# Spare products dropped, one copy moved and three tiles shifted at the start of a performer attention with a Mish network

## The chip, the cores and the metric

One Trainium2 chip, one core. The metric is the device time of one execution in microseconds, the median of several runs. The engines are TensorE (PE, matrix products), VectorE (DVE), ScalarE (ACT), GpSimd (POOL) and SyncE (SP), whose queue issues most of the transfers.

## The reference

Attention with random features ("performer"), 8 batches of 8 heads, 576 positions, 64 wide, 128 features; its output, one row of 512 for each of 4608 tokens, goes through a network with one hidden layer of 2048 and the activation Mish.

```python
def phi(x):
    h = einsum('bhsd,md->bhsm', x, omega) - sum(x * x, -1, keepdims=True) / 2.0
    return exp(h - max(h, -1, keepdims=True)) / sqrt(m)
q_p, k_p = phi(q * scale), phi(k * scale)
kv = einsum('bhsm,bhsd->bhmd', k_p, v)         # sums over the keys of a batch
num = einsum('bhsm,bhmd->bhsd', q_p, kv)
den = einsum('bhsm,bhm->bhs', q_p, sum(k_p, axis=2)) + 1e-06
x = (num / den) as 4608 x 512
out = mish(x @ w_in) @ w_out                   # mish(h) = h * tanh(log(1 + exp(h)))
```

## The kernel before, in words

The work is a stream of generators. Keys are handled by batch and pair of heads (`k_task`, tiles named k0_0 to k7_3), queries by tiles of 128 tokens (`q_task`, q0 to q35), both through `features`; the network goes by chunks of 256 tokens: `ff_in` for the first layer (PE tiles ph, 16 blocks of f each as ph chunk_group_quarter_pair), `ff_out0` and `ff_out` for the second (po). Weights arrive in eight blocks each (`w_task`), as raw words that ACT (Prelu), POOL and DVE turn into float32; a cast on ACT and a remainder on DVE (`w_split`) then give two float16 parts. `agenda` holds all generators with the slot at which they go on; `step` moves on to the next slot, and `yield n` puts a generator n slots back. What is written in that order is then placed by the Tile framework's scheduler, which gives every engine its order; `tc.high_priority(PRIO)` lets instructions be placed ahead of others. So a `yield 1` decides which rows stand beside each other, and the scheduler may move further ones.

The first tiles are special. Batches 0 and 1 and tiles 0 to 4 are computed in float32 (`whole`): ACT takes the exponentials straight from PSUM with `mx` as bias (L402), key sums are copied from PSUM into `kvf` (L461, by ACT), and `q_first` transposes the queries' features (pt, L581), copies them (qp, L584), multiplies them with the key sums (pn, L592) and divides (x, L599 or L605). Tiles 0 and 1 are transposed by PE (px, L616) into xT for chunk 0; tiles from 2 on are split (xs) and transposed by a DMA on SP (`x_parts`, L569). Tile 4 goes this way too; tiles from 5 on use float16 features in two parts (sq on ACT and POOL, pq L376 on PE, maxima and differences on DVE, exponentials L412 on ACT, qn on ACT and DVE, a transposing DMA to qp L525, pn L540).

`spin` (L97) puts products on PE that nobody reads. Thirteen of them open the kernel; `features` puts one or two behind the exponentials of the first tasks, counted by `nth` (0 to 3 are batch 0's keys, 4 and 5 are q0 and q1), and `q_first` puts two ahead of tile 0's last transposes.

Chunk 0's first layer leaves its sums in g (copied from ph by ACT), and `mish0` applies Mish to each half of g in place, 128x2048 at a time, the second half first as written. ACT must load a table of functions when it goes from exponentials or Prelu to Mish or back; these rows are ACT_TABLE_LOAD.

Transfers on SP go out in their order of issue. A load into a buffer waits until the last reader of that buffer is done: f buffers of tag `af` (queries and keys) rotate by two, raw buffers share the tag `g` with the hidden layers.

Of the kernel before, what the change touches and what calls it, by code (L numbers as in the profile page):

```python
# [15 lines left out]
AF = mybir.ActivationFunctionType  # L16
# [14 lines left out]
def tile_kernel(  # L31
# [17 lines left out]
    FT = DF // P  # L49
# [298 lines left out]
    def features(load, tiles, name, nth, whole):  # L348
# [61 lines left out]
        yield gap("exp", name)  # L410
        if not by_act:
            last = act.activation(e, e, AF.Exp, bias=lnt)  # L412
        elif nth < 6 and nth not in (2, 3):
            spin(2 if nth > 3 else 1, ident, e[:, 0:2, :].rearrange("p n m -> p (n m)"))
        anchors[nth] = anchors["e"] = (last.ins, sub.ins)
        return e

# [19 lines left out]
    def k_task(nth, b, hp):  # L437
# [8 lines left out]
        if b < KF:  # L446

            yield gap("kv", f"k{b}_{hp}")
            vt = vts[b]
            pkv = (ps_o if nth < 4 else ps_a).tile(  # L450
                [P, 2, D1], F32, tag="o" if nth < 4 else "a", name=f"pkv{b}_{hp}", padded_shape=[P, 2, 256]
            )
            for j in range(2):
                for i, (t, u) in enumerate(steps[j]):
                    nc.tensor.matmul(  # L455
                        out=pkv[:, j, :], lhsT=e[:, t, :], rhs=vt[hp][:, u, :],
                        start=i == 0, stop=i == 4,
                    )
            yield 1
            f = kvf[b][:, 2 * hp:2 * hp + 2]  # L460
            cast(act, f, pkv)  # L461
            did("kvf", b)
            yield 4
            if (b * S + S - 1) // P >= QF and hp == HP - 1:
                must(HP, "kvf", b)
                start(kv_parts(b, kvf[b], kv[b]))
            return
# [105 lines left out]

    def q_first(nth, t, e, off):

        qp = sb.tile([P, H, P], F32, tag="ap", name=f"qp{t}", bufs=2)
        for g in range(2):
            hs = slice(4 * g, 4 * g + 4)
            pt = ps_a.tile([P, 4, P], F32, tag="a", name=f"pt{t}_{g}")
            for i in range(4):  # L580
                nc.tensor.transpose(out=pt[:, i, :], in_=e[:, 4 * g + i, :], identity=ident)  # L581
            cast(act, qp[:, hs, :], pt)
        yield 1
        x = sb.tile([P, H, D], F32, tag="x", name=f"x{t}", bufs=2)  # L584
        rd = sb.tile([P, H, 1], F32, tag="rd", name=f"rd{t}")
        for g in range(2):
            hs = slice(4 * g, 4 * g + 4)
            pn = ps_a.tile([P, 4, D1], F32, tag="a", name=f"pn{t}_{g}", padded_shape=[P, 4, P])
            for i in range(4):
                for b, lo, hi in spans(t * P, P):  # L590
                    must(HP, "kvf", b)
                    nc.tensor.matmul(  # L592
                        out=pn[lo:hi, i, :], lhsT=qp[:, 4 * g + i, lo:hi], rhs=kvf[b][:, 4 * g + i, :],
                        start=True, stop=True,
                    )
            dve.tensor_single_scalar(out=rd[:, hs], in_=pn[:, :, D:D1], scalar=EPS, op=ALU.add)
            dve.reciprocal(out=rd[:, hs], in_=rd[:, hs])
            if t * P < CH:
                xt = dve.tensor_tensor(  # L599
                    out=x[:, hs, :], in0=pn[:, :, 0:D], in1=rd[:, hs].broadcast_to([P, 4, D]),  # L600
                    op=ALU.mult,
                )
                continue
            for b, lo, hi in spans(t * P, P):
                xt = dve.scalar_tensor_tensor(  # L605
                    out=x[lo:hi, hs, :], in0=pn[lo:hi, :, 0:D], scalar=vstate[b][2][lo:hi],
                    in1=rd[lo:hi, hs].broadcast_to([hi - lo, 4, D]), op0=ALU.mult, op1=ALU.mult,
                )
        anchors[30 + t] = (xt.ins,)
        if t * P >= CH:  # L610
            yield from x_parts(nth, t, x)
            return
        yield 1
        px = ps_a.tile([P, KT, P], F32, tag="a", name=f"px{t}")
        for i in range(KT):
            nc.tensor.transpose(out=px[:, i, :], in_=x[:, 2 * i:2 * i + 2, :], identity=ident)  # L616
        anchors[40 + t] = (cast(act, xT0()[:, :, off:off + P], px).ins, xt.ins)
        if off == 0:
            spin(2, ident, x[:, 0:4, :].rearrange("p h d -> p (h d)"))
        did("x0")  # L620


# [48 lines left out]
    def ff_in(c):  # L671
# [5 lines left out]
        for gr in range(FT // FG):  # L677
            gT[c, gr] = sb.tile([P, 2, FG, CH], F16, tag="g", name=f"g{c}_{gr}", bufs=GB)
            for q in range(FG // FQ):
# [4 lines left out]
                for j in range(0, FQ, 2):  # L684
# [11 lines left out]
                            )  # L696
                    if c == 0:

                        later(1, cast, act, h[:, j:j + 2, :], ph)
                        if gr == FT // FG - 1 and q == FG // FQ - 1 and j > 0:  # L700
                            later(2, mish0)
                    else:
# [53 lines left out]
    def mish(sp, h, ph):  # L756

        for us, lo, hi in sp:
            anchors["h"] = act.activation(h[:, :, lo:hi], ph[:, :, lo:hi], AF.Mish, scale=us[:, 0:1]).ins  # L759

    def mish0():
        for gr in reversed(range(FT // FG)):
            act.activation(g0(gr), g0(gr), AF.Mish)
            for q in range(FG // FQ):
                did("g", 0, q)

# [79 lines left out]
    def gap(what, name):  # L846
        if name in ("k0_0", "k0_1", "k0_2", "k0_3", "q0", "q1"):
            return GAP0[what]
        return GAP[what]

    def pace(c):
# [205 lines left out]
```

## Time and profile before

| | us |
|---|---|
| median of 3 runs (lowest to highest) | 938.64 (938.16 to 938.83) |
| the profiled execution | 937.79 |
| its span | 936.0 |
| PE busy, share of the span | 921.6, 98% |
| ACT busy | 628.5, 67% |
| DVE busy | 529.6, 57% |
| POOL busy | 231.1, 25% |

The profiled execution is one run, its span the time between the first and the last recorded instruction. Times below are from the span's start. A row of a timeline can hold several instructions of one form (xN) with its start, the time from the first's start to the last's end, and in brackets the idle time of the engine ahead of it and what ended that. Products in float32 leave two or more records each.

### The profile page before, as it was taken

The page shows a single profiled execution, that of the slowest core. Times are in us where ns is not written, and L with a number is a line of the kernel's source. Part 1 is how long each engine was busy: PE and PEld are TensorE (multiplying, and loading weights), DVE is VectorE, ACT ScalarE, POOL GpSimd, SP SyncE. Part 2 cuts the span into 40 slices and gives each one's busy share as a digit, 9 for nine tenths or more (in the row PEclk, how much of TensorE's full clock was granted, in tenths as well). Part 3 has the DMA queues.
Part 4 walks back from the last instruction along what each step waited for, and adds up shares of the span by engine and source line. Part 5 has one row for each costly group of instructions (what it writes and reads, how often), then busy time and mean ns, then how long its engine had stood idle before and what let it go on. Part 6 is the DMA issues. An engine that isn't in the chain of part 4 may idle for free.

```text
span 936.0 us, 16681 instructions
## 1 busy us (share of the span) xinstructions
PE 921.6 (98%) x6797; PEld 532.4 (57%) x6797; DVE 529.6 (57%) x1019; ACT 628.5 (67%) x914; POOL 231.1 (25%) x143
## 2 busy tenths in 40 slices
PE   9998999999999999999999999999999999999998
PEld 6886866777655555555555555555555555444443
DVE  3899779855646784577357753784476345201200
ACT  5769998996949954897388747963887268304401
POOL 1331143541432233313232232323332121000000
PEclk9999999999999999999999999999999999999999
DMA  9975334623531256214531264203430242101001
GB/s 284 327 210 180 112 70 96 119 86 71 133 94 37 52 122 122 61 28 98 109 89 38 47 128 120 49 24 77 117 50 23 46 113 43 37 1 46 1 1 45
DMA packets 128204, 82.05 MB, mean 88 GB/s; under 512 B 106432, under 2 KB 106560, under 8 KB 128128
## 3 DMA queue, kind: packets, MB, share of 16 engines
q1 hardware_dynamic: 127392, 79.47, 34.1%
q10 hardware_dynamic: 736, 1.52, 0.6%
q8 instruction: 53, 0.87, 0.4%
q14 instruction: 23, 0.19, 0.1%
HBM read 46.37 MB, written 9.44 MB: 60 GB/s over the span
## 4 chain that ended last, share of the span: by engine, by line
PE 89%; DVE 5%; ACT 4%; issue 1%; DMA 0%; POOL 0%; ACTq 0%; DVEq 0%; POOLq 0%
PE po L745 31%; PE ph L721 31%; PE po L787 6%; PE ph L692 5%; PE pq L376 3%; PE pk L376 2%; PE pkv L490 2%; PE pn L540 2%; PE pkv L455 2%; PE po L804 1%; PE spin L97 1%; DVE wmax L213 1%; DVE w L207 1%; PE pk L391 1%; ACT ek L402 1%
## 5 line engine op out<-in xcount | busy, mean ns | idle before, releaser
L721 PE MATMUL ph<-xT,w 128*128 128x512 f16 x1344 | 298.4, 379 | 0.0
L745 PE MATMUL po<-wo,gp 128*128 128x512 f16 x1344 | 296.9, 379 | 0.0
L745 PEld LDWEIGHTS <-gp 128*128 128x128 f16 x1344 | 129.5, 98 | 149.9
L721 PEld LDWEIGHTS <-w 128*128 128x128 f16 x1344 | 129.1, 98 | 148.2
L82 DVE SCALAR_TENSOR_TENSOR gp<-h,us,gp 128x256 f16<-128x256 f32 (+6 forms) x104 | 103.7, 1013 | 121.9 <-ACT gp L69 121.6
L759 ACT ACTIVATE h<-ph,us 128x128 f32<-128x128 f32 (+6 forms) x240 | 108.0, 502 | 46.5 <-PE ph L721 42.4
L78 POOL TENSOR_TENSOR sq<-fq,sq 64x1024 f16<-64x1024 f32 x31 | 67.0, 2163 | 213.9 <-ACT sq L69 118.0
L692 PE MATMUL ph<-xT,w 128*128 128x256 f16 (+2 forms) x720 | 96.4, 290 | 1.3 <-DMA xT<-xs 0.8
L69 ACT ACTIVATE o<-po,us 128x512 f32<-128x512 f32 (+1 forms) x38 | 25.9, 682 | 98.9 <-PE po L745 92.5
L78 POOL TENSOR_TENSOR xs<-x,xs 128x512 f16<-128x512 f32 x34 | 46.0, 1353 | 157.0 <-issue 80.0
L78 POOL TENSOR_TENSOR sk<-fk,sk 64x1152 f16<-64x1152 f32 x24 | 58.3, 2431 | 90.2 <-ACT sk L69 90.1
L397 DVE TENSOR_REDUCE mxk<-pk 128x4 f32<-128x512 f32 (+1 forms) x96 | 49.9, 549 | 45.9 <-PE pk L376 33.4
L69 ACT ACTIVATE gp<-h,us 128x256 f16<-128x256 f32 (+6 forms) x104 | 73.8, 755 | 0.3
L397 DVE TENSOR_REDUCE mxq<-pq 128x4 f32<-128x512 f32 x72 | 46.6, 680 | 43.6 <-PE pq L376 39.5
L787 PE MATMUL po<-wo,g 128*128 128x512 f16 x288 | 65.4, 379 | 0.0
L78 DVE TENSOR_TENSOR qn<-eq,qn 128x1024 f16<-128x1024 f32 x31 | 39.1, 1262 | 43.0 <-ACT qn L69 43.0
L692 PEld LDWEIGHTS <-w 128*128 128x128 f16 x576 | 55.5, 98 | 10.9 <-issue 2.4
L759 ACT ACT_TABLE_LOAD x43 | 55.2, 1283 | 0.8
L69 ACT ACTIVATE sq<-fq 64x1024 f16<-64x1024 f32 x31 | 32.7, 1055 | 31.4 <-issue 29.9
L412 ACT ACT_TABLE_LOAD x39 | 50.0, 1283 | 0.7
L78 DVE TENSOR_TENSOR kp<-ek,kp 128x1152 f16<-128x1152 f32 x24 | 33.9, 1414 | 25.1 <-ACT kp L69 25.1
L78 POOL TENSOR_TENSOR vb<-vf,vb 128x640 f16<-128x640 f32 x24 | 35.9, 1499 | 46.3 <-DVE vb L71 34.5
(127 smaller groups left out, 1063.1 us busy)
## 6 DMA issues: line engine op xcount, KB each, us to landing
vf<-in_vL_dram SPq DMA_DIRECT2D x30, 325.0 KB, 3.2
out_dram<-o SPq DMA_DIRECT2D x36, 256.0 KB, 2.3
fq<-in_qT_dram SPq DMA_DIRECT2D x31, 256.0 KB, 3.4
fk<-in_kT_dram SPq DMA_DIRECT2D x24, 256.0 KB, 3.6
raw<-in_w_out_dram SPq DMA_DIRECT2D x5, 1024.0 KB, 7.1
wo<-in_w_in_dram SPq DMA_DIRECT2D x4, 1024.0 KB, 12.3
raw<-in_w_in_dram SPq DMA_DIRECT2D x4, 1024.0 KB, 14.6
wo<-in_w_out_dram SPq DMA_DIRECT2D x3, 1024.0 KB, 8.3
```

Source lines behind the costliest of these rows:

```text
L69: return act.activation(out, in_, AF.Copy, scale=scale)
L78: ins = eng.tensor_tensor(out=out, in0=in_, in1=hi, op=ALU.subtract)
L82: return eng.scalar_tensor_tensor(out=out, in0=in_, scalar=scale, in1=hi, op0=ALU.mult, op1=ALU.subtract)
L376: nc.tensor.matmul(out=pp[:, i, :], lhsT=left[:, o:o + P], rhs=right, start=j == 0, stop=j == len(terms) - 1,)
L397: sub = dve.tensor_reduce(out=mx[:, lo:hi], in_=pp[:, :m, :], axis=AX.X, op=ALU.max, negate=by_act)
L412: last = act.activation(e, e, AF.Exp, bias=lnt)
L455: nc.tensor.matmul(out=pkv[:, j, :], lhsT=e[:, t, :], rhs=vt[hp][:, u, :], start=i == 0, stop=i == 4,)
L692: ff_mm[0] = nc.tensor.matmul(out=ph[:, i, part], lhsT=wi(a, k, f) if c else wi0(k, f), rhs=x_two(c // 2)[:, y, k, lo:lo + CH] if c else x ...
L721: ff_mm[0] = nc.tensor.matmul(out=ph[:, 0, :], lhsT=wi(a, k, f), rhs=x[:, y, k, :], start=n == 0, stop=n == len(mm) - 1,)
L745: ff_mm[0] = nc.tensor.matmul(out=po[i], lhsT=gP[g, gr][:, a, f % FQ, i * P:(i + 1) * P], rhs=wo(y, f), start=f == 0 and (a, y) == parts[0 ...
L759: anchors["h"] = act.activation(h[:, :, lo:hi], ph[:, :, lo:hi], AF.Mish, scale=us[:, 0:1]).ins
L787: ff_mm[0] = nc.tensor.matmul(out=po[i], lhsT=gT[c, f // FG][:, a, f % FG, i * P:(i + 1) * P], rhs=wo(y, f), start=f == order[0] and (a, y ...
```

## The change

Five edits. Tiles' products that nobody reads: `features` keeps one spin behind k0_0 and k0_1 and none behind q0 and q1, and `q_first` none ahead of tile 0's last transposes. The sum pkv0_3 of batch 0's last pair of heads is copied by DVE (`nth == 3`). `q_first` waits a step for t above 1, which holds for tiles 2, 3 and 4 (tiles 0 and 1 are not touched; tile 4 is the last that uses it). Tile 6's gap ahead of its products is 3 instead of 2. Chunk 0's Mish stands under high priority, as does the copy that fills the last block of its input, and the half of group 1 is done in two pieces of 128x1024.

```diff
-        elif nth < 6 and nth not in (2, 3):
-            spin(2 if nth > 3 else 1, ident, e[:, 0:2, :].rearrange("p n m -> p (n m)"))
+        elif nth < 2:
+            spin(1, ident, e[:, 0:2, :].rearrange("p n m -> p (n m)"))
...
-            cast(act, f, pkv)
+            cast(dve if nth == 3 else act, f, pkv)
...
     def q_first(nth, t, e, off):
 
+        if t > 1:
+            yield 1
...
-        if off == 0:
-            spin(2, ident, x[:, 0:4, :].rearrange("p h d -> p (h d)"))
         did("x0")
...
-                        later(1, cast, act, h[:, j:j + 2, :], ph)
+                        last = gr == FT // FG - 1 and q == FG // FQ - 1
+                        later(1, urgent if last else cast, act, h[:, j:j + 2, :], ph)
...
+    def urgent(*args):
+        with tc.high_priority(PRIO):
+            cast(*args)
+
     def mish0():
+        with tc.high_priority(PRIO):
+            mish0_()
+
+    def mish0_():
         for gr in reversed(range(FT // FG)):
-            act.activation(g0(gr), g0(gr), AF.Mish)
+            for q in ((1, 0) if gr else (slice(None),)):
+                w = g0(gr)[:, q * FQ:(q + 1) * FQ] if gr else g0(gr)
+                act.activation(w, w, AF.Mish)
...
         if name in ("k0_0", "k0_1", "k0_2", "k0_3", "q0", "q1"):
             return GAP0[what]
+        if what == "lo" and name == "q6":
+            return 3
         return GAP[what]
```

What the scheduler makes of it is seen in the built order of the engines. The first place is ACT around chunk 0's second Mish and the exponentials of batch 1's first keys (ek_0 is k1_0, ek_1 is k1_1, w_105 to w_109 are casts of weight blocks, raw_791 and raw_822 are Prelu). Before, from the cast that stands behind all of k1_0's exponentials:

```order
L69 ACTIVATE w_105<-w_106,s_w_656 128x1024
L198 ACTIVATE raw_791<-raw_791 128x1024
L402 ACTIVATE ek_1_824<-pk_1_5_828,mxk_1_825 128x128 x3
L69 ACTIVATE w_106<-w_107,s_w_656 128x1024
L402 ACTIVATE ek_1_824<-pk_1_0_826,mxk_1_825 128x128 x4
L402 ACTIVATE ek_1_824<-pk_1_5_828,mxk_1_825 128x128
L402 ACTIVATE ek_1_824<-pk_1_4_827,mxk_1_825 128x128
L69 ACTIVATE g_1_706<-ph_1_1_2_809 128x512
L69 ACTIVATE w_107<-w_108,s_w_656 128x1024
L198 ACTIVATE raw_822<-raw_822 128x1024
L763 ACT_TABLE_LOAD
L763 ACTIVATE g_1_706<-g_1_706 128x2048
```

And now, from the copy that is urgent:

```order
L69 ACTIVATE g_1_694<-ph_1_1_2_797 128x512
L69 ACTIVATE w_105<-w_106,s_w_644 128x1024
L774 ACT_TABLE_LOAD
L774 ACTIVATE g_1_694<-g_1_694 128x1024
L69 ACTIVATE w_106<-w_107,s_w_644 128x1024
L402 ACT_TABLE_LOAD
L402 ACTIVATE ek_0_760<-pk_0_0_762,mxk_0_761 128x128
L69 ACTIVATE w_107<-w_108,s_w_644 128x1024
L402 ACTIVATE ek_0_760<-pk_0_0_762,mxk_0_761 128x128 x2
L402 ACTIVATE ek_0_760<-pk_0_5_764,mxk_0_761 128x128 x4
L69 ACTIVATE w_108<-w_109,s_w_644 128x1024
L402 ACTIVATE ek_0_760<-pk_0_4_763,mxk_0_761 128x128
```

Mish moved ahead of eight of the nine exponentials of k1_0, with a table load on each side, and three casts between; the other piece of Mish stands further up, behind Mish of the other half. On PE the second layer of chunk 0 moved with it: four products po stand ahead of the rest of k1_1's products, three more behind the first pkv of batch 1, and then those of k1_2.

The second place is SP around tile 4's queries (fq_1069 before, fq_1058 now) and raw0 (raw_928, now raw_917); what an instruction waits for stands in brackets. Before:

```order
L170 DMA raw_898<-in_w_out_dram 128x2x512 [waits DMAHW6_49,DVE_49]
L321 DMA fq_1069<-in_qT_dram 64x512 [waits DMAHW2_49,DMAHW7_49,DMAHW1_49,PE_49]
L321 DMA fq_1069<-in_qT_dram 64x512 [waits DMAHW0_49]
L170 DMA raw_928<-in_w_out_dram 128x2x512 [waits DVE_49]
L290 DMA vf_2_1525<-in_vL_dram 128x650 [waits PE_49]
```

Now:

```order
L170 DMA raw_886<-in_w_out_dram 128x2x512 [waits DMAHW6_49,DVE_49]
L321 DMA fq_1058<-in_qT_dram 64x512 [waits DMAHW2_49,DMAHW7_49,DMAHW1_49,PE_49]
L170 DMA raw_917<-in_w_out_dram 128x2x512 [waits DMAHW0_49,DVE_49,Activation_49]
L321 DMA fq_1058<-in_qT_dram 64x512
L290 DMA vf_2_1514<-in_vL_dram 128x650 [waits PE_49]
```

raw0 went ahead of the second half of the queries and stands behind the first as before, whose wait on PE is for the products of k1_2, the last readers of its buffer.

The third place is ACT at tile 4 (eq its exponentials, qp the copies of its transposed features, sq the high part of tile 5's queries). Before:

```order
L402 ACT_TABLE_LOAD
L402 ACTIVATE eq_1111<-pq_0_1113,mxq_1112 128x128 x4
L402 ACTIVATE eq_1111<-pq_4_1114,mxq_1112 128x128 x4
L69 ACTIVATE g_0_867<-h_0_1_1027,us_862 128x1024
L69 ACTIVATE qp_1182<-pt_0_1183 128x512
L69 ACTIVATE qp_1182<-pt_1_1189 128x512
L759 ACT_TABLE_LOAD
L759 ACTIVATE h_1_0_1127<-ph_1_0_0_1128,us_862 128x512
L69 ACTIVATE sq_1252<-fq_1124 64x1024
L759 ACTIVATE h_1_0_1127<-ph_1_0_2_1196,us_862 128x512
```

Now:

```order
L402 ACT_TABLE_LOAD
L402 ACTIVATE eq_1100<-pq_0_1102,mxq_1101 128x128 x4
L402 ACTIVATE eq_1100<-pq_4_1103,mxq_1101 128x128 x4
L69 ACTIVATE g_0_855<-h_0_1_1016,us_850 128x1024
L760 ACT_TABLE_LOAD
L760 ACTIVATE h_1_0_1116<-ph_1_0_0_1117,us_850 128x512
L69 ACTIVATE sq_1210<-fq_1113 64x1024
L69 ACTIVATE qp_1197<-pt_0_1198 128x512
L69 ACTIVATE qp_1197<-pt_1_1204 128x512
L760 ACTIVATE h_1_0_1116<-ph_1_0_2_1172,us_850 128x512
```

The two copies moved behind a table load, a Mish and sq. On PE tile 4's products with the key sums (pn) stand ten products into the following block of the first layer instead of ahead of it, one product po more stands ahead of tile 5's pn, and half a block of chunk 1's second layer ahead of chunk 2's first product. Without the edit at tile 6 the built order is the same.

## Rows read from the trace of the kernel before

**Rows 1.** The page: its first line, and the granted clock of PE in 40 equal slices, in tenths of full speed (9 is 90% or more).

```profile
span 936.0 us, 16681 instructions
PEclk9999999999999999999999999999999999999999
```

**Rows 2.** Busy time by stretches: the stretch in us, its length, then busy time (and instructions) of PE, PE's weight loads, DVE, ACT, POOL, the granted clock, the mean busy share of the DMA engines, GB/s.

```profile
20.00:30.00 10.00, 10.00 (x95) 9.22 (x95) 4.91 (x7) 9.81 (x30) 4.21 (x4) 1.00 1.05 386
...
40.00:50.00 10.00, 8.73 (x73) 6.64 (x71) 9.86 (x24) 7.12 (x22) 0.52 (x1) 1.00 0.90 288
50.00:60.00 10.00, 10.00 (x60) 9.15 (x59) 10.00 (x20) 5.64 (x9) 2.88 (x2) 1.00 0.39 127
...
80.00:90.00 10.00, 8.10 (x70) 6.66 (x68) 9.19 (x12) 9.95 (x16) 0.00 (x0) 1.00 0.67 218
...
150.00:160.00 10.00, 9.16 (x85) 7.09 (x83) 9.86 (x28) 9.91 (x12) 4.46 (x2) 1.00 0.54 123
...
180.00:600.00 420.00, 420.00 (x3360) 237.26 (x3359) 259.47 (x507) 314.11 (x426) 125.70 (x71) 1.00 0.37 83
```

**Rows 3.** The waits of PE in the first 200 us, each with its line and with what ended it: us in total, times, the longest.

```profile
PE po L804 <- ACT g L763: 1.8, 1, 1.8
PE pk L376 <- DVE x L556: 1.6, 1, 1.6
PE spin L97 <- DVE idle L92: 1.5, 1, 1.5
PE pq L376 <- POOL sq L78: 1.5, 1, 1.5
PE pt L581 <- ACT eq L402: 1.3, 1, 1.3
PE pk L391 <- ACT ek L402: 1.1, 1, 1.1
PE ph L692 <- DMA xT<-xs: 0.8, 1, 0.8
```

**Rows 4.** The timeline of PE: start, time from the first's start to the last's end, line, operation, tiles and shapes.

```profile
27.21 1.03 PE L97 MATMUL spin<-eq,ident 128*128 128x256 f32 x4
...
29.64 3.24 PE L592 MATMUL pn<-kvf,qp 128*128 128x65 f32 x28
...
76.56 1.52 PE L391 MATMUL pk<-om_f,fk 64*128 64x128 f32 x18 [1.13 <-ACT ek L402]
...
80.10 2.34 PE L455 MATMUL pkv<-vf,ek 128*128 128x65 f32 x20
82.54 1.78 PE L391 MATMUL pk<-om_f,fk 64*128 64x128 f32 x20
...
88.84 5.42 PE L804 MATMUL po<-wo,g 128*128 128x512 f32 x12 [1.80 <-ACT g L763]
...
119.89 1.15 PE L592 MATMUL pn<-kvf,qp 128*64 128x65 f32 x32
...
154.80 2.75 PE L787 MATMUL po<-wo,g 128*128 128x512 f16 x12
```

**Rows 5.** The timeline of ACT.

```profile
75.90 1.64 ACT L402 ACTIVATE ek<-pk,mxk 128x128 f32<-128x128 f32 x6
77.48 1.15 ACT L69 ACTIVATE w<-w,s_w 128x1024 f16<-128x1024 f32 x1
...
85.58 1.28 ACT L763 ACT_TABLE_LOAD   x1
86.88 1.91 ACT L763 ACTIVATE g<-g 128x2048 f32<-128x2048 f32 x1
...
99.09 2.19 ACT L198 ACTIVATE raw<-raw 128x1024 f32<-128x1024 f32 x2
...
116.94 1.09 ACT L69 ACTIVATE qp<-pt 128x512 f32<-128x512 f32 x2 [0.25 <-PE pt L581]
...
119.34 0.69 ACT L759 ACTIVATE h<-ph,us 128x512 f32<-128x512 f32 x1
119.92 1.04 ACT L69 ACTIVATE sq<-fq 64x1024 f16<-64x1024 f32 x1
...
128.99 1.15 ACT L412 ACTIVATE eq<-eq,lnt 128x1024 f32<-128x1024 f32 x1
...
132.03 1.05 ACT L69 ACTIVATE qn<-eq 128x1024 f16<-128x1024 f32 x1
```

**Rows 6.** The timeline of DVE, where tile 4's products are divided, and at tile 5's differences.

```profile
120.62 0.16 DVE L596 TENSOR_SCALAR rd<-pn 128x4 f32<-128x4 f32 x1 [2.09 <-PE pn L592]
...
126.73 1.28 DVE L406 TENSOR_TENSOR eq<-pq,mxq 128x512 f32<-128x512 f32 x2
```

**Rows 7.** The issues on SP's queue (three rows of its timeline; the time is that of the issuing), and the median time from issue to landing of w_out's raw blocks, over the span and in 101 to 104 us.

```profile
84.36 1.84 SPq L321 DMA_DIRECT2D fq<-in_qT_dram  x2
87.16 0.37 SPq L170 DMA_DIRECT2D raw<-in_w_out_dram  x1
...
134.37 2.01 SPq L525 DMA_TRANSPOSE qp<-qn  x1
...
raw<-in_w_out_dram SPq DMA_DIRECT2D x5, 1024.0 KB, 7.1
...
raw<-in_w_out_dram SPq DMA_DIRECT2D x1, 1024.0 KB, 5.4
```

## The prediction

> **What bounds the kernel now.** I read the span and the granted clock first [rows 1], then the busy time of each engine by stretches [rows 2], then the list of TensorE's waits [rows 3]. The reader is to see a kernel with one tight engine and a ragged start: between 180 and 600 us TensorE (PE) is busy for 420.00 of 420 us at a clock of 1.00, which is 2.4 GHz, and it waits for nothing there. So whatever this change does, it does ahead of 180 us, and the place that PE has reached there is carried to the end. Ahead of it PE waits seven times for more than 0.7 us: 1.8 for the Mish of chunk 0, 1.6 for tile 7's quotient, 1.5 at the start, 1.5 for the low part of tile 6's queries, 1.3 for the exponentials of tile 2, 1.1 for those of batch 1's first keys, 0.8 for chunk 2's transposed input [rows 3]. Without the one at the start, that is 8.1 us.
>
> These waits are small because PE is not the only full engine. ScalarE (ACT) is busy 9.81 of 10 us in 20 to 30 and 9.95 in 80 to 90; VectorE (DVE) 9.86 in 40 to 50, 10.00 in 50 to 60, 9.86 in 150 to 160 [rows 2]. Where PE stops doing something there, it mostly waits sooner for the same result. I therefore read the timelines next [rows 4 to 6], to find which engine's row of work ends each wait, and last the transfers that this row needs [rows 7].
>
> The sum is made against the profiled execution, 937.79 us (span 936.0 and 1.79 around it); it lies 0.85 under the median of the runs, 938.64. I add the difference that I find to the median. About 0.2%, 1.9 us, is what a measurement of this kernel can tell from no change.
>
> **The change, part by part.**
>
> *The dropped products.* Three spins go, each of four records lasting 1.03 us or so [rows 4]; with the overlap of neighbours that is 2.6 us of PE's work. The first two stand where PE waits for tile 1's exponentials on an ACT that is full [rows 2]; their 1.7 us come back as a wait. The third stands ahead of the last transposes of tile 0, and what follows it soon meets DVE, full from 40 to 60. What is really won is a shorter tail of tile 0's and 1's products: 28 records are left behind the last transpose, 3.24 us or 0.116 each [rows 4], and 24 in the new order, so 0.46 us. The step later for tiles 2 and 3 puts a row of other products ahead of their transposes, a cover of 0.3 us for the 1.3 us wait. Bounds: nothing, and 2.6 us; I take 0.6 us won, by the row of 28, since the engine that ends the wait is full.
>
> *The copied key sum.* A copy of 128x130 leaves ACT for DVE, whose row begins only after an idle stretch. On ACT such a copy costs under 0.3 us. Cover: DVE's idle time ahead of tile 0's quotients. If that cover were gone it would cost the same 0.3 us. I take nothing; it is part of the 0.6 above.
>
> *Mish with priority.* Mish of half of chunk 0 (128x2048, 1.91 us [rows 5]) is cut into two pieces of about 0.96. The first stands beside Mish work of the other half and brings no table load; the second stands, by the new order of ACT, ahead of the exponentials of batch 1's first keys, between two table loads. PE gets its po products some 8 us sooner, but the exponentials come later. Before, they were done when the cast at 77.48 began [rows 5]. In the new order that cast, which can start no sooner since DVE's remainder of the block before it must be done, is followed by Mish (0.96) with two loads (2 x 1.28), three casts and eight exponentials. A cast takes 1.15 alone and 1.06 in a row (the overlap with the next is 0.09), an exponential 0.27 by the 1.64 of six: 1.06 + 2.56 + 0.96 + 3.18 + 2.16 = 9.9, so 87.4. PE, if it never waited, would be there at 85.5: from its start of po at 88.84 less the wait of 1.8, less pkv (2.34) and pk (1.7 without its overlap) that now follow, less 1.5 of pk and the 1.1 waited there, it reaches po at 80.4; four po of 0.9 (5.42 over six) and the 1.5 of pk bring 85.5 [rows 4]. It waits 1.9 in all where it waited 1.8 + 1.1 = 2.9 [rows 3]. So 1.0 us is won, with bounds of nothing (the two casts late by one more DVE step) and 2.9.
>
> The price of a table load decides here. The row shows a load at 85.58 for 1.28 us and Mish from 86.88, 0.02 us behind it [rows 5]. The Trainium skill (ScalarE: Activation LUTs, section "What ACT_TABLE_LOAD costs") counts 2.66 us for each switch, the load and a drain of 1.38. By that the exponentials would end 2.8 us later and the 1.0 won would be 1.8 lost. This trace does not show the drain as time of its own, and the row decides.
>
> *What the moved order does to a transfer.* raw0, a block of w_out of 1 MB, was issued at 87.16, behind both halves of tile 4's queries (84.36), and landed in 7.1 [rows 7], at 94.3; ACT took it behind 99.09 with no wait [rows 5]. Now batch 1's third key products stand behind po and the first pkv. The query load needs the buffer that these products read, and raw0 stands behind its first half on SP. Their end: 87.4 + 2.34 + three po (2.7) + 1.7 = 94.2; raw0 goes out at about 94.6 and lands at 101.7. Before, ACT had done with it at 99.09 + 2.19 = 101.3; now it can have done so 1.1 after the landing, at 102.8: 1.5 us late. Bounds: the shortest landing of such a block is 5.4 [rows 7], which leaves 100.0, but ACT's own work up to there (thirteen and a half us of casts, loads and exponentials behind 87.4) ends near 101.0, so 0.8 late at least; 2.5 at most, if the key products wait for their exponentials by another 1.0.
>
> *A step later takes tile 4 too.* The condition is t > 1, so tile 4 moves as well. On ACT its copies qp4 (116.94 to 118.03 [rows 5]) get a load, a Mish and sq5 put ahead of them: 1.28 + 0.69 + 0.95 = 2.9. With raw0's 1.5 they end at 118.03 + 4.4 = 122.4. Before, PE began pn4 at 119.89 [rows 4], 1.86 behind the copies, because it was in a block of the first layer; the new order puts pn4 inside the next block, so this slack goes: pn4 is 2.6 late. DVE waits for pn4 (idle 2.09 ahead of 120.62 [rows 6]) and everything behind it follows in one row: tile 5's maxima and differences, to 128.01. So eq5 is 2.6 late. ACT has 0.8 less between tile 5's exponentials and qn5 (before 130.14 to 132.03, a load and a Mish; now one cast, 1.06 [rows 5]). The transposing load of qp5, issued at 134.37 [rows 7], for which pn5 waits with nothing to spare, goes out 1.8 later; x5, its low part on POOL and xT1 follow at the same distance, and chunk 2's first product, which already waits 0.8 for xT1 [rows 3], begins 1.8 later. PE has 1.3 us more behind it by then: half of a po block of 2.75 [rows 4] is ordered ahead. Net 0.5 lost. The wait for tile 6's low part (1.5 [rows 3]) is gone, since PE arrives later; it is not counted, as xT1 ends last.
>
> *Afterwards.* Tile 7's quotient (1.6 waited for [rows 3]) hangs on DVE, busy 9.86 of 10 in 150 to 160 and 1.8 late from tile 5 on, while PE is only 0.5 late. That wait grows by nothing to 1.3; I take 0.5.
>
> *Tile 6's step.* The gap of 3 in place of 2 for tile 6's low part leaves the built order as it is without it: nothing.
>
> **The sum.** On the chain that ends last, xT1 and then tile 7's quotient, the change costs 0.5 + 0.5 = 1.0 us. The 0.6 and the 1.0 won earlier, and the 1.5 of tile 6, are spent waiting for xT1. Forecast: 938.64 + 1.0 = 939.6 us, no difference that can be told.
>
> **The rivals.**
>
> *Faster.* If raw0's load does not bind (0.8 late in place of 1.5) and DVE makes up the rest before qp5, by no more than the casts that stand between, then xT1 is not late and the gains stay: 0.6 + 1.0, and of tile 6's 1.5 what is not needed, at most 3.1. That is 935.5 to 937. For it: three waits of 1.3 to 1.8 are what the change aims its moves at. Against: ACT idles for only 0.05 of the 10 us from 80 to 90 [rows 2], so nothing there makes up anything.
>
> *Slower.* raw0 behind the query load on SP, with the key products waiting for the exponentials: 2.5 late instead of 1.5, and tile 7's wait grows by its whole 1.3. Then 0.5 + 1.0 + 1.3 = 2.8, 941.4; with the 0.8 of ACT not made up, 3.6, 942.2. It decides from a landing of raw0 later than 102.2. For it: 7.1 is the middle of five such loads [rows 7], the key products' place is hand-summed without any wait. Against: one block landed in 5.4.
>
> *The clock.* Without spins PE idles longer, about 2.5 us, near 27 and again near 45. In the rows PE's clock is 1.00 in every stretch, with a wait of 1.8 inside one [rows 1 to 3]. If it fell to 1.2 GHz, the 9 us of products between 25 and 35 would take twice that: 9 slower, 948. The Trainium skill (TensorE: Matmul & The Clock Gate, section on the HAM clock gate) says that an idle array falls back to half its clock, which speaks against dropping products that nobody reads. By the rows no idle stretch here did that. A chance of 0.02.
>
> *The change does nothing.* A scheduler sets the order; if the priority moved nothing, the time would be 938.6. The built order shows Mish and po moved, so this is only part of the middle case.
>
> **How the numbers follow.** The forecast with no difference that can be told, 0.47: its own range is 936.8 to 940.5. Faster, 0.20. Slower by the transfer, 0.31, and by the clock, 0.02. The range goes from 936.4, inside the faster case, to 942.2, the end of the slower one.
>
> **What would show it.** In the changed profile: PE waiting some 2 us near 27 and over 1 us for tile 2; po starting near 81; k1_0's exponentials done near 87.4; raw0 issued near 94.6 and ACT's Prelu waiting for it; pn4 near 122.5; qp5 issued near 136; over 1 us of wait for xT1 where 0.8 stood. I am wrong if raw0 goes out before 90, if PE's place at 180 us differs by over 2 us, or if the clock leaves 1.00.

## The result, and the profile after

The changed kernel takes 947.21 us (median of 6 executions, 942.69 to 951.35), the kernel before 938.57 beside it: a ratio of 1.0094, 95% interval 1.0074 to 1.0114. It is 8.6 us slower, outside the range. The executions of the same program spread over 8.7 us, those of the kernel before over 1.3.

The page of the profiled execution (950.84 us) shows the larger part of the reason in one line. First the span, then PE's granted clock in 40 slices, which answers to [rows 1]:

```profile
span 949.0 us, 16661 instructions
...
PEclk9799999999999999999999999999999999999999
```

The second slice has a 7 where all were 9. The windows give the stretches (length, busy time of PE, its weight loads, DVE, ACT, POOL, then the granted clock, the DMA share, GB/s):

```profile
24.00:29.00 5.00, 3.80 (x30) 3.14 (x29) 3.83 (x6) 5.00 (x16) 2.14 (x2) 1.00 1.05 387
29.00:40.00 11.00, 10.80 (x54) 10.13 (x54) 5.53 (x15) 4.50 (x9) 3.46 (x4) 0.53 1.04 337
86.00:91.00 5.00, 3.62 (x24) 1.75 (x22) 2.27 (x3) 4.99 (x12) 0.00 (x0) 1.00 0.01 3
91.00:98.00 7.00, 7.00 (x24) 5.45 (x25) 6.97 (x8) 6.98 (x15) 0.00 (x0) 0.51 0.36 103
148.00:152.00 4.00, 0.81 (x2) 0.00 (x0) 2.70 (x3) 2.22 (x3) 2.28 (x1) 1.00 0.69 131
152.00:156.00 4.00, 3.57 (x27) 2.44 (x28) 3.17 (x8) 2.10 (x2) 0.00 (x0) 0.57 0.30 74
...
180.00:600.00 420.00, 416.62 (x3357) 237.34 (x3356) 261.31 (x513) 314.40 (x423) 129.25 (x72) 1.00 0.38 85
```

PE is given half its clock three times (a fall, below), 0.53, 0.51 and 0.57 in the mean of these windows, 1.2 GHz instead of 2.4, and each time behind a stretch in which it had been busy for 3.80 of 5, 3.62 of 5 or 0.81 of 4 us. The clock missing is 11 x 0.47 + 7 x 0.49 + 4 x 0.43 = 10.3 us at full speed, of 13.0 by which this span is longer. From 180 us on the clock is whole again and PE as full as before but for 3.4 us of 420. These are two waits: 1.35 for a Mish at 181.38, and 2.03 at 187.49 for tile 7's quotient, which stood at 174.49 before (1.59). By there all of the 13.0 us have been lost.

What a fall costs stands in the timeline of PE, where [rows 4] had 3.24 us for 28 records of pn (0.116 each) and 2.34 for 20 of pkv:

```profile
25.79 1.04 PE L583 MATMUL pt<-ident,eq 128*128 128x128 f32 x8
28.04 1.36 PE L583 MATMUL pt<-ident,eq 128*128 128x128 f32 x5 [1.20 <-ACT eq L402]
...
30.90 5.22 PE L594 MATMUL pn<-kvf,qp 128*128 128x65 f32 x24
...
90.98 4.46 PE L455 MATMUL pkv<-vf,ek 128*128 128x65 f32 x20 [0.81 <-ACT ek L402]
...
129.66 1.15 PE L594 MATMUL pn<-kvf,qp 128*64 128x65 f32 x32
...
152.43 1.47 PE L540 MATMUL pn<-kv,qp 128*128 128x65 f16 x24 [3.63 <-DMA qp<-qn]
```

Now 24 records of pn take 5.22 us, 0.217 each, and 20 of pkv 4.46. The waits, which answer to [rows 3]:

```profile
PE pn L540 <- DMA qp<-qn: 3.6, 1, 3.6
PE pt L583 <- ACT eq L402: 2.6, 2, 1.4
PE pk L376 <- DVE x L556: 2.0, 1, 2.0
PE spin L97 <- DVE idle L92: 1.5, 1, 1.5
PE ph L692 <- ACT h L760: 1.4, 1, 1.4
PE pkv L455 <- ACT ek L402: 0.8, 1, 0.8
PE po L815 <- ACT g L774: 0.6, 1, 0.6
PE pk L391 <- ACT ek L402: 0.6, 1, 0.6
```

The long waits for Mish (1.8) and for tile 6's low part (1.5) are gone, as the change's moves promise; 3.6 us for tile 5's transposing load stand in their place, and several small ones around 84 to 91. ACT and SP at the predicted steps:

```profile
90.52 0.40 ACT L402 ACTIVATE ek<-pk,mxk 128x128 f32<-128x128 f32 x1
...
108.35 1.16 ACT L198 ACTIVATE raw<-raw 128x1024 f32<-128x1024 f32 x1 [0.87 <-DMA raw<-in_w_out_dram]
...
136.95 0.63 ACT L69 ACTIVATE xs<-x 128x512 f16<-128x512 f32 x1 [2.74 <-DVE x L607]
```

```profile
102.32 0.47 SPq L321 DMA_DIRECT2D fq<-in_qT_dram  x1
102.89 0.54 SPq L170 DMA_DIRECT2D raw<-in_w_out_dram  x1
...
148.10 1.99 SPq L525 DMA_TRANSPOSE qp<-qn  x1
```

k1_0's exponentials end at 90.9; raw0 goes out at 102.89, right behind the first half of tile 4's queries, and ACT waits 0.87 for it. Then ACT stands 2.74 us for tile 4's quotient, with tile 5's exponentials queued behind that row.

The six executions are a test by themselves. They are one program in one order, and their time goes for the most part with the mean clock: 942.69 us at 0.998, 945.00 and 946.39 at 0.996, 948.04 at 0.990, 950.84 at 0.989, 951.35 at 0.987. Taking (1 - clock) x span off each leaves 938.6 to 942.6, a mean of 940.4. By that, of the 8.7 us between the means some 6.9 are the clock's and 1.8 the order's. This counts all of the missing clock as lost time, which is too much: in e15 below two executions at 0.992 are 3.6 us behind the ten at 0.998 to 1.000, where the same product gives some 7. A straight line through the six points reaches 942.2 us at a clock of 1.00, which gives 5.2 to the clock and 3.5 to the order. The clock is given to three places, which is 0.5 us either way for one execution, so both splits are estimates.

### The profile page after: what moved, and what is told of

The parts are those of the page before. It is cut to its first block, busy times and chain, and to the rows that moved or that the text cites. A ratio compares the mean times of both kernels' runs of the same rounds, so it can differ in the third digit from the quotient of the medians.

```text
span 949.0 us, 16661 instructions
## 1 busy us (share of the span) xinstructions
PE 930.4 (98%) x6785; PEld 538.3 (57%) x6785; DVE 533.2 (56%) x1020; ACT 627.0 (66%) x912; POOL 227.8 (24%) x143
## 4 chain that ended last, share of the span: by engine, by line
PE 86%; DVE 5%; DMA 5%; ACT 2%; SPq 1%; issue 1%; POOL 0%; ACTq 0%; DVEq 0%; POOLq 0%
PE po L746 31%; PE ph L722 30%; PE po L798 6%; PE ph L692 5%; PE pq L376 3%; PE pn L540 2%; PE pkv L490 2%; PE pk L376 2%; PE po L815 2%; DMA raw<-in_w_in_dram 2%; DMA wo<-in_w_in_dram 2%; DMA qp<-qn 1%; PE pkv L455 1%; DVE wo L82 1%; DVE mxq L397 1%
## 5 line engine op out<-in xcount | busy, mean ns | idle before, releaser
L69 ACT ACTIVATE sq<-fq 64x1024 f16<-64x1024 f32 x31 | 32.8, 1058 | 31.2 <-issue 29.8
L69 ACT ACTIVATE xs<-x 128x512 f16<-128x512 f32 x34 | 21.3, 627 | 41.6 <-DVE x L556 33.5
```

The source lines that it names most:

```text
L69: return act.activation(out, in_, AF.Copy, scale=scale)
```

## The experiments

Theory A: the clock. Theory B: the order, with late transfers around tile 4. Times are medians against the kernel before on the same chip (938.25 to 938.60).

**The dropped products put back, in the changed kernel** (all six), and four of the six dropped from the kernel before:

```diff
 e1, in the changed kernel:
-        elif nth < 2:
-            spin(1, ident, e[:, 0:2, :]...)
+        elif nth < 6 and nth not in (2, 3):
+            spin(2 if nth > 3 else 1, ident, e[:, 0:2, :]...)
...
+        if off == 0:
+            spin(2, ident, x[:, 0:4, :]...)
 e2, in the kernel before:
-        elif nth < 6 and nth not in (2, 3):
-            spin(2 if nth > 3 else 1, ident, e[:, 0:2, :]...)
+        elif nth < 2:
+            spin(1, ident, e[:, 0:2, :]...)
```

> The changed kernel with all six dropped products put back (two behind each of q0's and q1's exponentials, two ahead of tile 0's last transposes). Theory A, the clock: the changed kernel loses time mostly because TensorE's clock falls to half (granted 0.50 from 29.8 to 39.5 us, again near 91 and near 153), the first time because nothing fills the wait for tile 1's exponentials. Then the clock stays at 1.00 from 25 to 40 and some 4.9 us come back: 941 to 943. Theory B, the order: the time is lost to late transfers around tile 4 and the clock's falls lie beside waits that are there anyway; then the products cost their 2.6 us of TensorE and the time stays at 946 to 949.

> The kernel before with only the products behind q0's and q1's exponentials dropped. Theory A: the clock falls to 0.50 at about 30 us for some 10 us, as in the changed kernel; 3 to 5 us slower than before, 941.5 to 943.5, and where the clock does not fall in an execution, no slower. Theory B: nothing behind 60 us is moved, so 938 to 939.

e1: 944.28 us, ratio 1.0066 (1.0054 to 1.0078). The clock, in the windows of the falls at 30 and 91:

```profile
29.00:40.00 11.00, 10.07 (x81) 8.96 (x80) 8.24 (x18) 6.93 (x12) 4.58 (x4) 1.00 1.06 345
91.00:98.00 7.00, 6.89 (x51) 4.81 (x51) 6.77 (x8) 6.98 (x15) 0.00 (x0) 1.00 0.67 225
```

Both falls are gone, and 2.9 us came back, not 4.9, so the time lies between the two theories: this kernel falls elsewhere, at 144 behind a wait of 2.03 us for tile 5's load, and from 178 to 186. The waits around Mish are still there (0.63 and 0.57 us, as in the changed kernel), and one of 1.98 at 78.9, with the clock whole. e2: 943.87 us, just above theory A's band, 1.0062 (1.0045 to 1.0078), executions from 941.63 at a clock of 0.998 to 946.66 at 0.991:

```profile
24.00:29.00 5.00, 3.82 (x30) 3.10 (x29) 3.32 (x4) 5.00 (x17) 2.80 (x2) 1.00 1.05 387
29.00:44.00 15.00, 14.31 (x71) 13.15 (x70) 8.11 (x18) 6.44 (x11) 4.46 (x4) 0.54 0.93 292
```

So dropping the four products brings the fall at 30 by itself, 15 x 0.46 = 6.9 us of clock in this execution. It falls once more, from 91 to 94, behind waits of 0.94 and 1.17 us for batch 1's exponentials. Less (1 - clock) x span an execution of e2 takes 937.3 to 939.8, but that the clock is all of the loss is not shown: e15 below, also without the four products, is 2.0 us slower than before with no fall in its profile.

**Mish alone, and the step later alone**, in the kernel before:

```diff
 e3: as in the change, urgent copy, priority, two pieces
+                        later(1, urgent if last else cast, act, h[:, j:j + 2, :], ph)
 e4:
     def q_first(nth, t, e, off):
+        if t > 1:
+            yield 1
```

> The kernel before with only the urgent copy, the priority and Mish in two pieces. Theory A: po runs sooner, but TensorE then waits two or three times between 84 and 92 us for exponentials; if the fall of the clock near 91 belongs to this part, it is seen here too (granted 0.50 for some 6 us) and the time is 1 to 3 us above before. Theory B: the part is worth my 1.0 us: 937.5 to 938.5, clock 1.00.

> The kernel before with only the step later for tiles 2, 3 and 4. Theory A: tile 5's transposing load is late, TensorE waits over 2 us for it near 150 and the clock falls behind that; 2 to 4 us slower, 940.5 to 942.5. Theory B (the step as I predicted it, net of other waits): 939.1 to 940.1, clock 1.00.

e3: 943.38 us, 1.0056 (1.0044 to 1.0068), above the 1 to 3 us of theory A. My 1.0 us won is refuted; the fall is there, behind waits of 0.97 and 0.66 us for exponentials, and a second one at 178, behind 1.41 for a Mish and 2.21 for tile 7's quotient:

```profile
82.00:86.00 4.00, 3.25 (x33) 2.88 (x34) 2.88 (x5) 4.00 (x8) 0.00 (x0) 1.00 0.09 23
86.00:90.00 4.00, 4.00 (x11) 1.84 (x10) 3.65 (x4) 4.00 (x12) 0.00 (x0) 0.57 0.68 214
178.00:182.00 4.00, 3.67 (x16) 1.75 (x17) 3.86 (x11) 3.97 (x5) 2.08 (x2) 0.57 0.68 180
```

e4: 944.38 us, 1.0053 (1.0039 to 1.0067). It costs more than A expected, and at another place than both theories had it: not near 150, but at 80.5, where PE waits 3.59 us for k1_0's exponentials, since a weight cast ahead of them on ACT waits for DVE. The clock falls behind it, and again at 180. PE, then ACT:

```profile
80.55 2.48 PE L391 MATMUL pk<-om_f,fk 64*128 64x128 f32 x18 [3.59 <-ACT ek L402]
```

```profile
75.42 1.15 ACT L69 ACTIVATE w<-w,s_w 128x1024 f16<-128x1024 f32 x1 [2.92 <-DVE w L82]
```

**Products that nobody reads added at the two falls that e1 left:**

```diff
+    def fill(n, out):
+        for _ in range(n):
+            nc.tensor.matmul(out=out, lhsT=om[:, 0, :], rhs=om..., start=True, stop=True)
...
+                if name == "k2_1" and pp is pps[0][0]:
+                    fill(12, pp...)
...
+                if t == 5 and g == 0:
+                    fill(14, pn[:, :, 0:D])
```

> The changed kernel with the six dropped products back and, beside them, 14 products that nobody reads ahead of tile 5's pn and 12 ahead of the key products of k2_1, about 1.5 and 1.3 us, at the two places where the clock still fell with the six products back (waits of 2.0 and 1.3 + 1.3 us, falls at 144 and 178). Theory A, the clock: the waits that are left are too short, the clock stays at 1.00 up to 200 us, and 3.4 us (two falls of 1.71) come back: 940 to 941.5. Theory B, the order: the fillers cost what they take where they don't fit the wait; 944 to 947.

942.72 us, 1.0048 (1.0036 to 1.0061), clock 0.998 to 1.000. The clock held, but only 1.6 us came back, between the two theories; e1's two falls were 1.7 and 3.4 us of clock in its profile, 5.1 and not 3.4. The fillers take 1.70 and 1.47 us, and waits are left, the longest 2.16 us for chunk 2's transposed input at 153.9. So this order of work, with its fillers and without any fall, is still some 4 us slower than before.

**The small parts alone**, in the kernel before:

```diff
 e6:
-            cast(act, f, pkv)
+            cast(dve if nth == 3 else act, f, pkv)
 e7:
+        if what == "lo" and name == "q6":
+            return 3
 e8:
-        if off == 0:
-            spin(2, ident, x[:, 0:4, :]...)
```

> The kernel before with only the last key sum of batch 0 copied by VectorE. Theory A: a time above 940 only with a granted clock below 1.00; if ScalarE's full stretch around 25 to 30 us gets shorter, tile 1's exponentials come sooner and it is the same as before, 938 to 939. Theory B (what my walk through the order gave for the moves that this copy sets off): 941 to 942 with the clock at 1.00.

> The kernel before with only tile 6's gap of 3 steps. Theory A: time follows the clock; if the wait for tile 6's low part (1.5 us) goes and no other passes 2 us, the clock is 1.00 and the time is 937 to 938.5. Theory B: the step is worth nothing, as I predicted, 938.4.

> The kernel before with only the two products ahead of tile 0's last transposes dropped. Theory A: the wait for tile 0's transposed input (0.47 us at 34.9) grows by up to 0.9 us and stays under 2, so the clock holds at 1.00: 937.5 to 938.6. Theory B: any dropped product lets the clock fall: 940 or more.

e6: 942.94 us, 1.0048 (1.0034 to 1.0062). e7: 938.28, 0.9997 (0.9988 to 1.0006). e8: 938.39, 0.9996 (0.9987 to 1.0006). Tile 6's step and tile 0's products are free. The copy of 0.3 us, which I took for nothing, costs 4.4, with the clock below 1.00 as theory A has it, and not where it stands (26.10 on DVE): PE reaches tile 2's transposes at 45.62, where it did so at 45.41 before. The timeline of PE in e6, then the clock:

```profile
79.08 1.52 PE L391 MATMUL pk<-om_f,fk 64*128 64x128 f32 x18 [1.14 <-ACT ek L402]
...
81.41 2.45 PE L455 MATMUL pkv<-vf,ek 128*128 128x65 f32 x20 [0.48 <-ACT ek L402]
85.01 3.21 PE L391 MATMUL pk<-om_f,fk 64*128 64x128 f32 x20 [1.16 <-ACT ek L402]
```

```profile
84.00:92.00 8.00, 6.99 (x42) 5.47 (x43) 7.44 (x9) 7.97 (x13) 0.00 (x0) 0.57 0.68 212
```

Three waits of 1.14, 0.48 and 1.16 us for exponentials, and a fall. The timeline of DVE tells why:

```profile
71.87 1.22 DVE L213 TENSOR_REDUCE wmax<-wo 128x1 f32<-128x1024 f32 x1
...
74.33 0.68 DVE L397 TENSOR_REDUCE mxk<-pk 128x4 f32<-128x512 f32 x1
```

And before:

```profile
72.21 0.69 DVE L397 TENSOR_REDUCE mxk<-pk 128x4 f32<-128x512 f32 x1
...
75.05 1.21 DVE L213 TENSOR_REDUCE wmax<-wo 128x1 f32<-128x1024 f32 x1
```

The maximum of a weight block (1.22 us) now stands ahead of the maxima of k1_0's products, which come at 74.33 where they came at 72.21 before. The edit made the scheduler turn two rows.

**Which of the products, which tiles, and the two free parts together**, in the kernel before:

```diff
 e9:
+        if 1 < t < 4:
+            yield 1
 e10 (q0's dropped):
-        elif nth < 6 and nth not in (2, 3):
+        elif nth < 6 and nth not in (2, 3, 4):
 e11 (q1's dropped):
-        elif nth < 6 and nth not in (2, 3):
+        elif nth < 5 and nth not in (2, 3):
 e12: the edits of e7 and e8
```

> The kernel before with the step later for tiles 2 and 3 alone (tile 4 as before). Theory of the prediction: the cost sits with tile 4, whose products and tile 5's transposing load are late; without tile 4 the time is 938 to 939 at a clock of 1.00. Rival, from the step alone for 2, 3 and 4: there TensorE waits 3.6 us at 80.5 for exponentials behind a cast that waits for VectorE, and the clock falls behind that; tiles 2 and 3 are what stands on VectorE ahead of it, so the wait, the fall and 942 to 945 stay.

> The kernel before with only the two products behind q0's exponentials dropped (those behind q1's stay). The clock's theory: the wait ahead of tile 1's transposes is cut in two pieces, each under 1.3 us, with a product between; if that holds the clock, no fall at 30 and 938 to 939; if all four are needed, a fall at about 30 us and 941 to 944.

> The kernel before with only the two products behind q1's exponentials dropped (those behind q0's stay). TensorE then has its wait of 1.2 us or more in one piece right ahead of tile 1's transposes. The clock's theory: a fall at about 30 us in most executions, as with all four dropped, 941 to 944; if the one piece is too short, 938 to 939.

> The two parts that did no harm by themselves, together: the kernel before with the products ahead of tile 0's last transposes dropped and tile 6's gap of 3. The clock's theory: no wait over 2 us, clock 1.00, 937.5 to 938.5, as before or 0.1% faster. Rival (any reordering costs): over 940.

e9: 943.28 us, 1.0055 (1.0040 to 1.0071): tiles 2 and 3 alone do what e4 did, with a wait of 2.28 us at 79 and a fall from 80 to 83.5. Tile 4, on which the prediction put the cost, is not needed. e10: 943.52, 1.0053 (1.0039 to 1.0067); e11: 942.26, 1.0042 (1.0028 to 1.0056). The times are in the band of a fall at 30, but neither profile falls there, so the reason that the band was given for is refuted. Both fall later, e10 from 87 to 91 behind the three waits of e6 (1.14, 0.48, 1.18), e11 from 84 to 91.5 with one of 1.16 at 84; in both, as in e2 and e6, the maximum of the weight block stands ahead of k1_0's maxima. e12: 937.68, 0.9987 (0.9978 to 0.9996): the lowest median, 0.9 us under the kernel before, and no wait over 1.8 us.

**The turned rows bound back.** The maximum of block 6 is bound behind k1_0's maxima; with the copy (e13), with q1's products dropped (e14), with all four dropped (e15), and with e12 and the copy (e16):

```diff
-        if n == 0:
-            yield W_MAX[i]
-        with behind((AM, AO)[n][i]):
+        if n == 0 or i == 6:
+            yield W_MAX[i] if n == 0 else 1
+        with behind("mk" if n and i == 6 else (AM, AO)[n][i]):
...
+        if name == "k1_0":
+            anchors["mk"] = (sub.ins,)
```

> The kernel before with the key sum copied by VectorE, and the maximum of weight block 6 of w_out (1.2 us on VectorE) bound to come behind the maxima of k1_0's key products, as it does in the kernel before; with the copy alone it came ahead of them. Theory: that turn of the scheduler's order is what the copy costs; it makes k1_0's exponentials 2 us late, TensorE waits three times between 79 and 85 us and the clock falls. Bound back, no fall and 938 to 939.5. Rival: the copy's own shift at 26 to 37 us does it; 941 to 943 as without the binding.

> The kernel before without the two products behind q1's exponentials, with the same binding. Same theory: 938 to 939.5 and clock 1.00 (without the binding 942.3). Rival: the dropped products themselves cost it: 941 to 943.

> The kernel before without the four products behind q0's and q1's exponentials, with the same binding. With VectorE's order bound, the fall of the clock near 30 us, seen with all four dropped, is left alone. If it costs what its half time is (a fall from 29.5 to 40 or 43 is 5 to 7 us at half speed), 943 to 945; if VectorE, full from 44 to 75, takes most of that up, 939 to 941; if the fall does not come in some executions, those are at 938.

> The parts that do no harm: the products ahead of tile 0's last transposes dropped, tile 6's gap of 3, the key sum copied by VectorE, with the binding. Without copy and binding this was 937.7. Theory: clock 1.00, no wait over 2 us, 937 to 938. Rival (the copy still tips something): over 940.

e13: 938.76 us, 1.0004 (0.9995 to 1.0012). Of the copy's 4.4 us 0.5 are left, which can't be told from nothing. Its DVE, PE and clock, to be read against e6's:

```profile
72.35 0.68 DVE L397 TENSOR_REDUCE mxk<-pk 128x4 f32<-128x512 f32 x1
...
75.06 1.21 DVE L213 TENSOR_REDUCE wmax<-wo 128x1 f32<-128x1024 f32 x1
```

```profile
76.55 1.52 PE L391 MATMUL pk<-om_f,fk 64*128 64x128 f32 x18 [0.75 <-ACT ek L402]
...
88.83 3.70 PE L806 MATMUL po<-wo,g 128*128 128x512 f32 x8 [1.78 <-ACT g L765]
```

```profile
84.00:92.00 8.00, 6.22 (x36) 3.85 (x37) 6.34 (x8) 7.94 (x7) 0.00 (x0) 1.00 0.86 317
```

One wait of 0.75 in place of three, and the clock is whole, though the wait of 1.78 for Mish is back. e14: 939.80, 1.0018 (1.0009 to 1.0027), 2.5 us better than e11, 0.3 above its band; 1.5 stay. e15: 940.26, 1.0025 (1.0015 to 1.0035), 3.6 better than e2. Ten of its 12 executions take 938.92 to 940.62 at 0.998 to 1.000, two take 943.74 and 943.89 at 0.992. That is the band of a fall that DVE makes up for, but the profile shows none, and without a fall I had expected 938. PE's timeline in the profile, one of the ten:

```profile
28.37 1.36 PE L583 MATMUL pt<-ident,eq 128*128 128x128 f32 x5 [1.18 <-ACT eq L402]
...
30.65 2.79 PE L594 MATMUL pn<-kvf,qp 128*128 128x65 f32 x24
...
46.52 0.66 PE L583 MATMUL pt<-ident,eq 128*128 128x128 f32 x4 [1.98 <-ACT eq L402]
```

The same wait of 1.18 us at the same place as in e2 and in the changed kernel (1.20), and pn at full speed. The wait of 1.98 stands in e14 too:

```profile
45.67 0.66 PE L583 MATMUL pt<-ident,eq 128*128 128x128 f32 x4 [2.00 <-ACT eq L402]
```

There the clock falls behind it (0.57 from 46 to 50), in e15 it does not. So the length of a wait does not decide alone whether the clock falls, and the 2 us that several expectations go by are no limit. What e15 loses without a fall is order: PE, with four products less to do, is at tile 2's transposes at 46.52 instead of 45.41 and at Mish's po at 90.97 instead of 88.84. e16: 939.11, 1.0005 (0.9997 to 1.0014), in neither band: with the copy, bound, e12's 0.1% is gone.

Does the turn stand in the changed kernel? Its DVE:

```profile
80.05 0.29 DVE L397 TENSOR_REDUCE mxk<-pk 128x1 f32<-128x128 f32 x1
80.25 1.21 DVE L213 TENSOR_REDUCE wmax<-wo 128x1 f32<-128x1024 f32 x1
```

It does not: the maximum of the weight block stands behind k1_0's maxima, as before. In e1, e5, e17 and e18 it is turned (74.12 ahead of 77.45 in e1). So this turn, which is what the copy costs alone, is no part of the 8.6 us, and the runs from e1's kernel carry a turn that the changed kernel lacks. A binding was not tried in them.

**Tile 4, and all three tiles, put back in e1's kernel:**

```diff
 e17:
-        if t > 1:
+        if 1 < t < 4:
             yield 1
 e18:
-        if t > 1:
-            yield 1
```

> The changed kernel with all six dropped products back and the step later for tiles 2 and 3 alone. Theory: tile 4's place is what makes qp5 late; with it back, the wait of 2.0 us for qp5 and the fall at 144 go, 941 to 942.5 (944.3 with tile 4 a step later). Rival: the chain is late from batch 1's exponentials on, whatever tile 4 does: 943.5 to 945.

> The changed kernel with all six dropped products back and no tile a step later, so Mish, the copy and tile 6 are left of the change. Theory: what Mish alone gave with the clock's falls (943.4) plus what the copy gave (4.4) do not add up, since both make the same exponentials late: 942 to 944, clock about 0.996. Rival (they add): 946 to 948.

e17: 943.77 us, 1.0059 (1.0044 to 1.0074), inside the rival's band: the wait of 2.0 for qp5 and the fall at 144 go, and a wait of 2.23 for xT1, without a fall, and a fall at 178 come. e18: 941.76, 1.0037 (1.0027 to 1.0046), under both bands and near the first: the parts do not add up. Without the late steps 2.6 us of e1's 5.9 come back, and most of its executions hold the clock.

## Why the prediction was wrong

**The step that failed is that the clock stays at 1.00.** Forecast, range and chances rest on it, and the rival called the clock got 0.02, with 948 us; 947.2 is what came. That the two are so near is luck: the rival had one fall, of 9 us; in the profile that fall, from 29.8 to 39.5, is some 5.2 us of clock, two later falls that it did not have are as much again, waits are added, and the executions range from 942.69 to 951.35. I had reasoned that a wait of 1.8 us stands in the trace before with the clock at 1.00, so that no idle stretch here brings it down. e15 against e2, and the six executions of the changed kernel, show that such a row holds for its own surroundings only: 1.2 us at 28 brought the fall in the profiles of e2 and of the changed kernel and, by their clocks, not in ten of twelve executions of e15, and in e13 a wait of 1.78 us is harmless where in e6 three of 0.5 to 1.2, near each other, are not. That nearness is what counts is not shown: e18 and e17 do the same work around xT1, with waits of 0.44 and 2.04 us and of 0.45 and 2.23, and the clock falls behind them in e18 and not in e17. The Trainium skill (TensorE: Matmul & The Clock Gate, section on the HAM clock gate) says that an array that idles falls back to half its clock; the trace agrees, 0.53 from 29 to 40 us. I let the row decide against the rule, and the row did not reach that far.

**The dropped products.** Predicted 0.6 won. Measured: e2, 5.5 lost; e15, 2.0 lost with DVE's order bound and no fall in its profile. So the bounds, nothing and 2.6 won, were wrong even with a whole clock: more came back as waits than the products took. I counted them as work; they also keep PE busy, and dropping them moves the order (block 6's maximum is turned in e2, e10 and e11). That the third pair wins nothing was right (e8).

**The copy.** Predicted nothing, measured 4.4 (e6), of which e13 takes 4 back: its price alone is the order that it turns, not its 0.3 us. In the changed kernel these rows are not turned.

**Mish.** Predicted 1.0 won, measured 5 lost (e3). The sum was right in its mechanism: exponentials later, 87.4 predicted and 90.9 measured with the first fall ahead of it. It counted 1.9 us of wait against 2.9, and the changed kernel has 2.0 there (0.63, 0.57 and 0.81). What it left out is the fall behind them, and in e3 the waits and the fall at 172 to 182. The table load went as the row had it: 1.28 us and the next instruction 0.02 behind.

**raw0 and tile 4.** raw0 did go out behind the query load, at 102.89 instead of 94.6, and ACT waited 0.87 for it (101.7 less 101.0, or 0.7, in the prediction's numbers). For pn4 I had 122.5, measured 129.66; for qp5's issue 136.2, measured 148.10. From pn4 to that issue it is 18.4 us where it was 14.5, and I had 13.7: tile 4's quotient comes late on DVE, and ACT waits 2.74 us for it in front of tile 5's exponentials. The wait that counted there was not xT1's (0.49, where I had over 1) but qp5's, 3.63. The last was tile 7's quotient, as predicted, 0.44 longer where I had 0.5. Yet in the experiments tile 4 was not the main cost: tiles 2 and 3 were. I had taken them for a cover of 0.3 us; alone they cost 4.7 (e9), with a wait for k1_0's exponentials and a fall behind it. And e17 without tile 4 was no better than e1 beyond the noise.

**Tile 6.** Nothing predicted, nothing measured (e7). In the kernel before the step does move rows, though: tile 7's quotient is waited for 0.95 us instead of 1.59.

**The sum.** With the clock taken out, 1.8 to 3.5 us of the changed kernel are the order's, more than the 1.0 predicted. That is a difference of readings, not a run. Executions with a clock of 0.999 or 1.000 point the same way: e5's take 942.3 to 943.0 with its fillers, e18's 940.5 to 942.4, e15's 938.9 to 940.6. The parts don't add up to the whole: alone, the four products cost 5.5, the copy 4.4, Mish 5.0 and the step later 6.0, 20.9 together, and the change 8.6. What share of it is Mish's and what the late steps' stays open, as does why the same wait brings a fall in one execution and none in the next.

## What to carry to other kernels

A kernel that is full on PE lives by its clock: before taking out products that nobody reads, or moving a wait, count each new wait of a us or more as a risk, and after it look at the clock of every execution, not only at busy shares. Which wait brings a fall no row here told ahead. Where a scheduler sets the order, an edit's price is the order that comes out: alone, the copy of 0.3 us cost 4.4 by turning two rows 46 us later, and binding them gave 3.9 back. Such a price need not come along into a larger change, which can turn the rows back. Two parts of the change were free, and together a little faster; measured singly they would have been found at once.

## What was not expected of the hardware

A wait's length does not tell whether the clock falls: with the same 1.2 us of idle at 28 us it fell in e2's profile and not in e15's, with 2.0 at 46 in e14's and not in e15's, and the same program took 942.69 to 951.35 us at mean clocks of 0.998 to 0.987. Missing clock is not lost time one for one: some 7 us of it cost 3.6 in e15. While the clock was down, pn's records took 0.217 us against 0.116.
